# An adaLN block with an S4 convolution and a SwiGLU FFN on one core: K's rows in float32, the gate row's sum ahead of the FFN, and two moves around the first FFN step

## The chip, the core and the metric

The kernel runs on one core of a Trainium2 chip. The core has five engines, each with its own queue of instructions: TensorE (PE; its weight loads are listed apart as PEld), VectorE (DVE), ScalarE (ACT), GpSimd (POOL) and SyncE (SP), which here only issues DMAs. PE reads its operands from the on-chip memory SBUF and writes to the accumulator memory PSUM, which has eight banks. The engines wait for one another through semaphores.

The metric is the device time of one execution in microseconds (us), the median of several runs. A profiled execution has a time of its own, and a span from its first to its last instruction. Times below are us from that span's start unless they are said to be whole executions.

## The reference, cut to what matters

The input is x with 2048 rows (tokens) and 448 columns (channels). A row vector c gives six rows of 448 by `silu(c) @ w_mod`: shift, scale and gate (sa, ca, ga) for the first branch and (sb, cb, gb) for the second.

```python
mod = (_silu(c) @ w_mod).reshape(c.shape[0], 6, 1, -1)
sa, ca, ga, sb, cb, gb = (mod[:, 0], mod[:, 1], mod[:, 2], mod[:, 3], mod[:, 4], mod[:, 5])
h = _layernorm(x, axis=-1) * (1 + ca) + sa
x = x + ga * _A_ref(h, ...)      # convolution along the rows, one filter K[d, l] per channel, plus h * Dskip
h = _layernorm(x, axis=-1) * (1 + cb) + sb
x = x + gb * _B_ref(h, w_gate, w_up, w_down)   # (silu(h @ w_gate) * (h @ w_up)) @ w_down
```

The filter is `K[d, l] = Re(sum over n of C[d, n] exp(dt[d] A[d, n] l) dt[d] B[d, n])` for lags l from 0 to 2047, with 256 states n per channel.

## The kernel before, in words

**Tiles and blocks.** The 2048 rows are 16 tiles of 128, taken in six blocks of 2, 2, 3, 3, 3 and 3 tiles. For each block the FFN runs over 14 chunks of 128 hidden columns (steps 0 to 13, `gate_up(f, nw)` at L753 to L786). A step multiplies the block's normalized rows, held with channels on partitions, by the gate and up weights of its chunk, takes SiLU of the gate part on ACT (`p`, L768), multiplies on DVE (L781) and splits the product into a high and a low float32r part (`phi`, L784; `plo`, L785). `down(f - 1)` (L797) then adds the chunk before times its down weights into one PSUM bank per tile, DN[0] to DN[2]. Every float32 operand of these products is a high part rounded to float32r plus a low part with the remainder; products of high with low and low with high are added.

**Block 0 is fresh.** In it the weights arrive by DMA and are split, two steps ahead: `split_w` for the gate and up weights (high part on ACT, L123; two subtractions on DVE, L125 and L127), `split_d` for the down weights (ACT L115, DVE L117). DMA buffers for raw weights are freed by those subtractions. In steps 0 and 1 the products stand in an order by which high parts come first and low parts last.

**The first branch.** If a flag computed from A, dt and the length says that the exponents stay small, K's rows are taken as a value plus lag times a slope, one row each (k0, k1); the convolution is then a triangular matrix of ones times h * k0 plus a matrix of lag ramps times h * k1, and what passes from tile to tile is a running row (`run`). Otherwise a general path is taken, which this input does not take; after the flag all engines branch.

**The preamble.** Before the first FFN step the kernel does everything for tiles 0 and 1: six modulation rows by PE from w_mod, the sums over states for K's value and slope (DVE products, ACT sums), K's rows, the convolution of tiles 0 and 1, their second layer normalization, the transposes that put channels on partitions, and the first two weight splits. The order is written out by hand: the string PLAN is a list of names, and each name issues one small function, so the order of names is the order in every engine's queue. The names that this document uses:

- `m0`, `m1`: K's value and slope, four columns of 128 channels. `k0`, `k1` spread them to rows over all partitions (`row_of`, L371), `gdr` does so for the gated skip. `gc0`, `gc1` copy the rows to SBUF.
- `v00` to `v11`: h times k0 (v0) or k1 (v1) for tiles 0 and 1; `o00` to `o14`: their products on PE into DN[0] and DN[1], two accumulators that are the tiles' branch outputs; `hd1`, `xh1`: tile 1's skip part.
- `cp`/`ck`/`cbw`, `sp`/`sbt`/`sbc`: the rows cb and sb, summed as four groups of partitions (quads), then spread (`ck`) or turned to columns.
- `st`, `r`, `n1`, `xn`, `tr`, `hi`, `lo` with 0 or 1: for tiles 0 and 1 the second norm's statistics (DVE), reciprocal root (POOL, L167 and L168), centring (DVE), scaling (ACT, L519), transposes (PE, L391 and L394), high parts (ACT, L457) and low parts (DVE, L462).
- `w0`, `w01`, `w02`, and `w1`, `w11`, `w12`: the split of the gate and up weights of chunks 0 and 1 into high part (ACT) and two subtractions (DVE); `d00`, `d01`: the down weights of chunk 0.
- `l1`: two products whose sum the running row needs (L434); `lr0`, `lr1`: the running row's copy, sum (L439) and the small DMA that puts it in place (ACT's queue, L440); `x0`: the copy of tile 0's branch output out of DN[0].

**The gate row gb** is not in PLAN: `end_gate` runs in FFN steps 1 and 2 of block 0, five quad products (L248, L251) into the bank CV, a copy to SBUF, a spread by one product (L259) and a second copy.

Of the kernel before, what the change touches and what calls it, by code (L numbers as in the profile page):

```python
# [43 lines left out]
o10 m1 k1 cpc gd h11 hd0 v01 ck sq0 v10 cbw o12 v11 w0 o01 o02 hd1 o13 o14 xh1 gc0 sa st0 fs sp r0 n10 spc x1 xn0 gc1 st1 sbt tr0 sbc r1  # L44
fl n11 l1 hi00 xn1 w01 tr1 hi01 w02 hi1 lo0 lo1 w1 w11 d00 w12 lr0 d01 x0 lr1"""
# [11 lines left out]
def tile_kernel(ctx, tc, x, a_re, a_im, b_re, b_im, c_re, c_im, log_dt,  # L57
# [198 lines left out]
    def end_gate(z):  # L256

        if z:
            pe.matmul(CV[:, 0:D], pick.to_broadcast([128, 128]), gb, start=True, stop=True)  # L259
        else:  # L260
            mod_quads(CV, gate_w)
        sc.copy(gb, CV[:, 0:D])

# [13 lines left out]
    with tc.tile_pool(name="pre", bufs=1) as pre:  # L277
# [72 lines left out]
        ms = [pre.tile([128, 2, 4], F32R, name=f"ms{q}") for q in range(2)]  # L350
        gd2 = pre.tile([128, 2, 4], F32R, name="gd2")
# [10 lines left out]
        def parts_of(o, m, en):  # L362
            en.tensor_copy(o[:, 0], m)
            en.tensor_tensor(o[:, 1], m, f32(o[:, 0]), op=OP.subtract)

        def row_of(m, ps, last=ident2):

            for k in range(4):
                n = 128 if k < 3 else 64
                for z in range(2):  # L370
                    pe.matmul(ps[:, k * 128:k * 128 + n], m[:, z, k:k + 1].to_broadcast([128, 128]),  # L371
                              identr if k < 3 else last, start=z == 0, stop=z == 1)
# [29 lines left out]
        def gd_row():  # L402
            psm["d"] = bank()
            row_of(gd2, psm["d"], identr[:, 0:64])

        def scaled(o, a, b):
            po.tensor_tensor(o, a, b, op=OP.add)
            po.tensor_tensor(o, o, gac, op=OP.mult)
            parts_of(ms[0], o, po)

        def slope_of():
            ve.tensor_tensor(m1, a1, a2, op=OP.add)
            parts_of(ms[1], m1, ve)

        def gated_skip():
            po.tensor_tensor(gdm, vec[:, 8:12], gac, op=OP.mult)
            parts_of(gd2, gdm, po)
# [18 lines left out]
        def left_rows(z):  # L436
            e = slice(96, 128)
            if z:
                ve.tensor_tensor(run0[e], run1[e], os[1][e], op=OP.add)  # L439
# [19 lines left out]
        def low(q):  # L459
            for k in range(4):  # L460
# [13 lines left out]
        def flag_of():  # L474
# [18 lines left out]
            "m0": do(scaled, m0, m0, m0_), "m1": slope_of, "dg": gated_dt, "dga": gated_slope,  # L493
            "k0": do(row_of, ms[0], CV), "k1": do(row_of, ms[1], DN[2]), "gdm": gated_skip, "gdr": gd_row, "gd": copy(gd, lambda: psm["d"][:, 0:D]),
# [3 lines left out]
            **{n: do(quads, n[0], g) for n, g in (("gp", 2), ("cp", 4), ("sp", 3))},  # L498
# [5 lines left out]
            "cbw": lambda: sc.activation(cbw, psm["c"][:, 0:D], AF.Identity, bias=1.0),  # L504
            "sbt": lambda: turned_to(psm["s"], qt["s"]), "sbc": do(columns, sbc, "s"),
# [9 lines left out]
            "l1": left_over, **{f"lr{z}": do(left_rows, z) for z in range(2)}, "xh1": do(skip, 1), "x1": branch_1,  # L515
# [6 lines left out]
            **{f"lo{q}": do(low, q) for q in range(2)},  # L522
            "x0": copy(xs[0], os[0]),
# [200 lines left out]

    def gate_0():
# [3 lines left out]
    def run_blocks(pools, stages, first=None):  # L729
# [144 lines left out]
        for b, ts in enumerate(TILES):  # L874
            todo = {}
            if b + 1 < len(TILES):
# [221 lines left out]
```

## Time and profile before

| | |
|---|---|
| median of 3 runs | 491.31 us (489.86 to 491.55) |
| the profiled execution | 490.08 us |
| its span | 488.1 us |
| granted TensorE clock, mean over the span | 0.992 |
| PE busy | 97% of the span |
| DVE, ACT, POOL busy | 58%, 32%, 13% |
| chain that ended last | PE 93%, DMA 2%, ACT, DVE, POOL and issue 1% each |

The busy shares are means over the span. PE's records are pipelined and their ends are modelled, so two records that overlap don't mean two products at once; what a product costs is read from the start of one to the start of the next. A row of a timeline reads: start, length, engine, line, operation, output and input tiles, shape, how many in a row, and in brackets the engine's idle time before it with what ended that. The chain lists pieces with their start, length, engine, tile and line.

The span falls in three parts: the preamble up to about 35 us, block 0 of the FFN (14 steps of 3.8 us), and the five other blocks, in which PE is the bound. DMA is busy at 90% or more of its share up to the third slice of 12 us; the loads that the preamble reads are all issued at its start.

### The profile page before, as it was taken

How to read it: one execution, taken by the hardware profiler on the slowest of the kernel's cores; microseconds unless marked ns; L12 is line 12 of the kernel's file. 1: busy time of each engine (PE TensorE's matmuls, PEld its weight loads, DVE VectorE, ACT ScalarE, POOL GpSimd, SP SyncE). 2: the span in 40 equal slices, each digit the busy share in tenths (PEclk: the TensorE clock that was granted, in tenths of full speed). 3: DMA queues.
4: the chain of work that ended last, by engine and by line, in shares of the span. 5: the costliest groups of instructions: out<-in, count | busy, mean ns of one | idle time of the engine just before them, and what ended most of it. 6: DMA issues, size and time to landing. Idle time of an engine off the chain costs nothing.

```text
span 488.1 us, 7029 instructions
## 1 busy us (share of the span) xinstructions
PE 475.0 (97%) x2743; PEld 447.4 (92%) x2743; DVE 285.3 (58%) x553; ACT 155.5 (32%) x336; POOL 61.5 (13%) x86
## 2 busy tenths in 40 slices
PE   6979999999999999999999999999999999999996
PEld 4648988999998999999999999999999999999995
DVE  5877999777886536565554657364475635222225
ACT  5765645532225112232212233231222241211111
POOL 1330000000000040410004131002241000000000
PEclk9988999999999999999999999999999999999999
DMA  8953663020000200011120011130001112000001
GB/s 312 405 210 106 197 201 120 19 95 1 0 3 1 94 1 0 24 42 45 59 77 0 2 43 45 43 109 6 2 0 45 44 43 77 21 1 0 1 1 62
DMA packets 18778, 31.24 MB, mean 64 GB/s; under 512 B 2608, under 2 KB 13488, under 8 KB 18736
## 3 DMA queue, kind: packets, MB, share of 16 engines
q1 hardware_dynamic: 18000, 30.52, 18.6%
q8 instruction: 23, 0.38, 0.3%
q10 hardware_dynamic: 736, 0.19, 0.2%
q14 instruction: 19, 0.16, 0.1%
HBM read 24.61 MB, written 6.03 MB: 63 GB/s over the span
## 4 chain that ended last, share of the span: by engine, by line
PE 93%; DMA 2%; ACT 1%; DVE 1%; POOL 1%; issue 1%; DVEq 0%; POOLq 0%
PE bank L753 59%; PE dn L797 27%; DMA wm<-in_w_mod_groups_dram 2%; DMA vec<-in_c_log_dt_dram 1%; PE dn L753 1%; PE dn L483 1%; PE bank L959 1%; PE cv L958 0%; PE cv L960 0%; ACT sca L360 0%; PE bank L972 0%; POOL rsb L168 0%; DVE x L836 0%; PE bank L206 0%; PE cv L971 0%
## 5 line engine op out<-in xcount | busy, mean ns | idle before, releaser
L753 PE MATMUL bank<-hhi,gu 128*128 128x384 f32 (+1 forms) x1169 | 212.1, 320 | 0.0
L753 PEld LDWEIGHTS bank<-hhi,gu 128*128 128x128 f32 x1169 | 192.0, 189 | 3.1 <-issue 0.7
L753 PE MATMUL bank<-hlo,gu 128*128 128x384 f32 (+1 forms) x668 | 132.0, 320 | 0.0
L753 PEld LDWEIGHTS bank<-hlo,gu 128*128 128x128 f32 x668 | 110.5, 189 | 0.0
L781 DVE TENSOR_TENSOR bank<-raw,bank 128x384 f32<-128x384 f32 (+1 forms) x69 | 36.9, 534 | 125.4 <-PE bank L753 122.1
L784 ACT CAST phi<-bank 128x384 fp32r<-128x384 f32 (+1 forms) x83 | 36.8, 444 | 141.4 <-DVE bank L781 141.4
L768 ACT ACTIVATE raw<-bank 128x384 f32<-128x384 f32 (+1 forms) x70 | 32.8, 469 | 123.1 <-PE bank L753 117.1
L785 DVE TENSOR_TENSOR plo<-bank,phi 128x384 fp32r<-128x384 f32 (+1 forms) x83 | 42.4, 511 | 37.1 <-ACT phi L784 37.1
L797 PE MATMUL dn<-wdh,phi 128*128 128x448 f32 x218 | 58.3, 369 | 0.0
L797 PE MATMUL dn<-wdh,plo 128*128 128x448 f32 x218 | 57.8, 366 | 0.0
L797 PE MATMUL dn<-wdl,phi 128*128 128x448 f32 x218 | 57.6, 365 | 0.0
L797 PEld LDWEIGHTS dn<-wdl,phi 128*128 128x128 f32 x218 | 41.0, 188 | 3.4
L797 PEld LDWEIGHTS dn<-wdh,plo 128*128 128x128 f32 x218 | 40.9, 188 | 3.3
L797 PEld LDWEIGHTS dn<-wdh,phi 128*128 128x128 f32 x218 | 38.8, 188 | 2.6 <-ACT run L982 0.7
L167 POOL TENSOR_SCALAR rsb<-mvb 128x1 f32<-128x1 f32 (+2 forms) x13 | 4.6, 354 | 173.4 <-DVE mvb L151 173.4
L167 POOL TENSOR_SCALAR rsa<-mva 128x3 f32<-128x3 f32 (+1 forms) x6 | 2.4, 396 | 119.2 <-DVE mva L151 119.2
L123 ACT CAST gu<-raw 128x1024 fp32r<-128x1024 f32 x14 | 14.6, 1046 | 0.0
L125 DVE TENSOR_TENSOR gu<-raw,gu 128x768 fp32r<-128x768 f32 x14 | 13.3, 951 | 0.5 <-ACT gu L123 0.5
L933 POOL TENSOR_TENSOR m<-m,gm 128x448 f32<-128x448 f32 x9 | 10.4, 1155 | 21.4 <-DVE m L184 17.5
L947 DVE TENSOR_TENSOR vl<-m,vh 128x448 fp32r<-128x448 f32 x12 | 9.1, 756 | 6.7 <-ACT vh L946 6.1
L194 ACT ACTIVATE raw<-raw,rsb 128x64 f32<-128x64 f32 x14 | 4.8, 346 | 21.0 <-DVE raw L193 11.9
L952 POOL TENSOR_TENSOR m<-m,gd 128x448 f32<-128x448 f32 x9 | 11.5, 1282 | 0.0
(243 smaller groups left out, 418.8 us busy)
## 6 DMA issues: line engine op xcount, KB each, us to landing
raw<-in_B_w_gate_up_dram SPq DMA_DIRECT2D x14, 512.0 KB, 3.7
rawd<-in_B_w_down_dram SPq DMA_DIRECT2D x16, 224.0 KB, 4.0
x<-in_A_u_dram SPq DMA_DIRECT2D x12, 224.0 KB, 2.9
out_dram<-x SPq DMA_DIRECT2D x11, 224.0 KB, 2.0
xd<-raw SPq DMA_DIRECT2D x9, 256.0 KB, 2.0
raw<-xd SPq DMA_DIRECT2D x36, 64.0 KB, 1.9
wm<-in_w_mod_groups_dram SPq DMA_DIRECT2D x5, 448.0 KB, 8.2
wm<-in_w_mod_groups_dram SPq DMA_DIRECT2D x5, 336.0 KB, 8.2
```

The source lines that it names most:

```text
L123: sc.copy(wgu[j][:, :, 0:4, :], w)
L125: en.tensor_tensor(lo, w[:, :, 0:3, :], f32(hi), op=OP.subtract)
L167: po.tensor_scalar(rs[:, 0:n], self.mv[:, 0:n, 1], EPS, None, op0=OP.add)
L753: pe.matmul(ps[s][:, 0:n], w[:, s, a], (hlo if lo else hhi)[:, k, 0:n], start=first and q == 0, stop=end and q == len(ka) - 1)
L768: sc.activation(p[:, 0:n], ps[0][:, 0:n], AF.Silu)
L781: ve.tensor_tensor(ps[1][:, 0:n], p[:, 0:n], ps[1][:, 0:n], op=OP.mult)
L784: sc.copy(hi[:, 0:n], ps[1][:, 0:n])
L785: ve.tensor_tensor(lo[:, 0:n], ps[1][:, 0:n], f32(hi[:, 0:n]), op=OP.subtract)
L797: pe.matmul(dn[q][:, 0:D], u[:, cs], v, start=f == 0 and z == 0, stop=f == (NF - 3 if last else NF - 1) and z == 2)
L933: (ve if on_v else po).tensor_tensor(v, h, g, op=OP.mult)
L947: ve.tensor_tensor(vl, v0, f32(vh), op=OP.subtract)
L952: (ve if on_v else po).tensor_tensor(h, h, gd, op=OP.mult)
```

## The change: what it does

- **K's rows in float32.** `row_of` takes the four columns and the identity as they are, in float32, one product per group of 128 channels. Before, each column was split into a high and a low float32r part (`parts_of`: two operations, on POOL for k0 and the skip, on DVE for k1), and each group took two products with a float32r identity. The splits and the float32r identity go.
- **The gate row's sum ahead of the FFN.** `end_gate` goes. PLAN has `gq` (the five quad products, into a bank of their own), `qtb` (the copy), `gbk` (the spread) and `gb` (the second copy).
- **First weights split ahead of the second root.** `w0` moves ahead of `cbw` on ACT, and `w01`, the long subtraction, ahead of `hd1` on DVE. `w02` stays behind tile 1's centring.
- **Running row and first tile's copy inside the first FFN step.** `lr0`, `lr1` and `x0` leave PLAN; `first_rows` does the same in FFN step 0, behind `gate_up(0)` and ahead of `gate_0`.
- **Smaller moves.** `o10`, the product of v0 with a matrix of ones, goes behind `k1` and `ck`; `d00` and `d01` ahead of `w1` and `w11`; tile 0's low parts are issued in two halves.

```diff
-o10 m1 k1 cpc gd h11 hd0 v01 ck sq0 v10 cbw o12 v11 w0 o01 o02 hd1 o13 o14 xh1 gc0 sa st0 fs sp r0 n10 spc x1 xn0 gc1 st1 sbt tr0 sbc r1
+m1 k1 cpc gd h11 hd0 ck v01 sq0 o10 v10 w0 cbw o12 v11 w01 o01 o02 hd1 o13 o14 xh1 gc0 sa st0 fs sp gq r0 n10 spc x1 xn0 gc1 st1 sbt tr0
...
-    def end_gate(z):
-
-        if z:
-            pe.matmul(CV[:, 0:D], pick.to_broadcast([128, 128]), gb, start=True, stop=True)
-        else:
-            mod_quads(CV, gate_w)
-        sc.copy(gb, CV[:, 0:D])
...
-        ident2 = pre.tile([128, 64], F32R)
-        identr = pre.tile([128, 128], F32R)
-        ve.tensor_copy(identr, ident)
+        ident2 = pre.tile([128, 64], F32)
...
-        def parts_of(o, m, en):
-            en.tensor_copy(o[:, 0], m)
-            en.tensor_tensor(o[:, 1], m, f32(o[:, 0]), op=OP.subtract)
-
...
-                for z in range(2):
-                    pe.matmul(ps[:, k * 128:k * 128 + n], m[:, z, k:k + 1].to_broadcast([128, 128]),
-                              identr if k < 3 else last, start=z == 0, stop=z == 1)
+                pe.matmul(ps[:, k * 128:k * 128 + n], m[:, k:k + 1].to_broadcast([128, 128]), ident if k < 3 else last,
+                          start=True, stop=True)
...
-        def left_rows(z):
-            e = slice(96, 128)
-            if z:
-                ve.tensor_tensor(run0[e], run1[e], os[1][e], op=OP.add)
-                sc.dma_start(run[0:1], run[127:128])
-            else:
-                sc.copy(run1[e], CV[e, 0:D])
...
+            "qtb": copy(gb, lambda: psm["gq"][:, 0:D]), "gb": copy(gb, lambda: psm["gq"][:, 0:D]),
+            "gbk": lambda: pe.matmul(psm["gq"][:, 0:D], pick.to_broadcast([128, 128]), gb, start=True, stop=True),
...
+    def first_rows():
+
+        e = slice(96, 128)
+        sc.copy(run1[e], CV[e, 0:D])
+        sc.copy(xs[0], DN[0][:, 0:D])
+        ve.tensor_tensor(run0[e], run1[e], DN[1][e, 0:D], op=OP.add)
+        sc.dma_start(run[0:1], run[127:128])
+
...
                     go(EXTRA[0], gate_0)
-                    go(2, end_gate, 0)
-                    go(4, end_gate, 1)
+                    at(0, 0, first_rows)
```

How the rows stand in the engines' queues (line numbers are each kernel's own; the names after the operation are output and inputs):

PE, from K's value row to the spread of cb. `cv` takes k0, the first `bank` the skip row, `dn_70` is DN[2] with k1, `dn_68` and `dn_69` are the two tiles' accumulators. Before:

```order
L371 MATMUL cv<-identr,ms_257 128x128 x6
L371 MATMUL cv<-ident_181,ms_257 128x64 x2
L371 MATMUL bank<-identr,gd_259 128x128 x6
L371 MATMUL bank<-identr,gd_259 128x64 x2
L248 MATMUL bank<-wm_140,cs 32x448 x3
L251 MATMUL bank<-wm_140,cs 32x224 x2
L483 MATMUL dn_68<-v_0_245,tri 128x448
L513 MATMUL dn_69<-v_0_245,all_178 128x448
L371 MATMUL dn_70<-identr,ms_258 128x128 x6
L371 MATMUL dn_70<-ident_181,ms_258 128x64 x2
L400 MATMUL bank<-qtc,pick 128x448
```

The same place after:

```order
L354 MATMUL cv<-ident,m_233 128x128 x3
L354 MATMUL cv<-ident_181,m_233 128x64
L354 MATMUL bank<-ident,gdm 128x128 x3
L354 MATMUL bank<-ident,gdm 128x64
L248 MATMUL bank<-wm_140,cs 32x448 x3
L251 MATMUL bank<-wm_140,cs 32x224 x2
L449 MATMUL dn_68<-v_0_243,tri 128x448
L354 MATMUL dn_70<-ident,m_237 128x128 x3
L354 MATMUL dn_70<-ident_181,m_237 128x64
L383 MATMUL bank<-qtc,pick 128x448
L481 MATMUL dn_69<-v_0_243,all_178 128x448
```

Each row has four products for eight, and the product with all ones stands behind the slope's row and cb's spread.

DVE, from tile 0's second statistics to the weights of chunk 0 (`gu_146`). Before:

```order
L481 TENSOR_TENSOR hd_250<-h_244,gd 128x448
L150 BN_STATS stb<-dn_68 128x6
L151 BN_AGGR mvb<-stb 128x2
L466 SCALAR_TENSOR_TENSOR h_0_251<-dn_68,mvb,cbw 128x448
L452 TENSOR_TENSOR x_73<-dn_69,hd_250 128x448
L150 BN_STATS stb<-x_73 128x6
L151 BN_AGGR mvb<-stb 128x2
L397 TENSOR_REDUCE sbc<-bank 128x4
...
L466 SCALAR_TENSOR_TENSOR h_1_252<-x_73,mvb,cbw 128x448
L125 TENSOR_TENSOR gu_146<-raw,gu_146 128x2x384
L127 TENSOR_TENSOR gu_146<-raw,gu_146 64x2x128
```

And after:

```order
L447 TENSOR_TENSOR v_1_246<-h_242,dn_70 128x448
L125 TENSOR_TENSOR gu_146<-raw,gu_146 128x2x384
L447 TENSOR_TENSOR hd_248<-h_242,gd 128x448
L150 BN_STATS stb<-dn_68 128x6
L151 BN_AGGR mvb<-stb 128x2
L432 SCALAR_TENSOR_TENSOR h_0_249<-dn_68,mvb,cbw 128x448
L418 TENSOR_TENSOR x_73<-dn_69,hd_248 128x448
L150 BN_STATS stb<-x_73 128x6
L151 BN_AGGR mvb<-stb 128x2
```

The long subtraction stands ahead of tile 1's skip part, not behind its centring. The two rows left out in the first piece make the flag.

PE, from the shift row to the transposes of tile 1. Before, the five gate quads stand in step 1 (`cv<-m_79`):

```order
L248 MATMUL bank<-wm_143,cs 32x448 x3
L251 MATMUL bank<-wm_143,cs 32x224 x2
L391 MATMUL bank<-ident,qts 128x128 x3
L394 MATMUL bank<-ident,qts 64x128 x2
L391 MATMUL bank<-ident,h_0_251 128x128 x3
L394 MATMUL bank<-ident,h_0_251 64x128 x2
L434 MATMUL cv<-v_0_247,all_178 128x448
L434 MATMUL cv<-v_1_248,all_178 128x448
L391 MATMUL bank<-ident,h_1_252 128x128 x3
...
L753 MATMUL bank<-hlo,gu_148 128x256 x8
L248 MATMUL cv<-m_79,cs 32x448 x3
L251 MATMUL cv<-m_79,cs 32x224 x2
```

After:

```order
L248 MATMUL bank<-wm_143,cs 32x448 x3
L251 MATMUL bank<-wm_143,cs 32x224 x2
L248 MATMUL bank<-m_79,cs 32x448 x3
L251 MATMUL bank<-m_79,cs 32x224 x2
L374 MATMUL bank<-ident,qts 128x128 x3
L377 MATMUL bank<-ident,qts 64x128 x2
L374 MATMUL bank<-ident,h_0_249 128x128 x3
L377 MATMUL bank<-ident,h_0_249 64x128 x2
L408 MATMUL cv<-v_0_245,all_178 128x448
L408 MATMUL cv<-v_1_246,all_178 128x448
L472 MATMUL bank<-gb,pick 128x448
L374 MATMUL bank<-ident,h_1_250 128x128 x3
```

The gate's quads follow the shift's, and its spread stands between the running row's products and tile 1's transposes. On ACT the running row's copy, tile 0's copy and the DMA stood ahead of the branch to the FFN; they stand behind the first step's high part now, ahead of the next down weight's cast. On DVE the running row's sum stands behind step 0's low part and the third weights' subtractions.

More of the change, by code (lines that the diff above doesn't have):

```diff
@@ L403, in gd_row @@
             psm["d"] = bank()
[L404 removed]
+            row_of(gdm, psm["d"], ident[:, 0:64])
         def scaled(o, a, b):
@@ L1031, in tile_kernel @@
     with cond.Else():
-        for z in range(2):
-            end_gate(z)
         y = general_conv()
```

27 lines of the change are left out of this document (9 added, 18 removed).

## The prediction

> **What bounds the kernel now.** I read the page's shares and clock row first, then windows cut where the clock changes, then the chain that ended last, and last the timelines of single engines. Times are us from the span's start.
>
> ```profile
> PE 475.0 (97%) x2743; PEld 447.4 (92%) x2743; DVE 285.3 (58%) x553; ACT 155.5 (32%) x336; POOL 61.5 (13%) x86
> ...
> PEclk9988999999999999999999999999999999999999
> ```
>
> TensorE (PE) is the bound nearly everywhere, and its product count hardly changes. What can change is the start: the third and fourth slices (24 to 49 us) are where the granted clock sags. The windows of that place, and one from earlier (columns: stretch, its length, busy time of PE, PEld, DVE, ACT and POOL with their instructions, granted clock, DMA share, GB/s):
>
> ```profile
> 8.88:12.29 3.41, 2.14 (x6) 0.86 (x6) 2.71 (x4) 1.44 (x5) 0.93 (x2) 1.00 1.03 412
> 29.36:32.77 3.41, 1.99 (x15) 1.01 (x13) 2.87 (x8) 1.65 (x5) 2.06 (x2) 1.00 0.08 30
> 32.77:36.19 3.42, 2.58 (x12) 1.88 (x13) 1.51 (x6) 2.30 (x8) 0.00 (x0) 0.50 0.56 153
> 36.19:39.60 3.41, 3.41 (x18) 3.41 (x18) 3.28 (x7) 2.03 (x4) 0.00 (x0) 0.50 0.19 23
> 39.60:43.02 3.42, 3.42 (x34) 3.12 (x34) 0.92 (x2) 1.84 (x4) 0.00 (x0) 1.00 0.36 132
> ```
>
> From 32.77 to 39.60 PE runs at half clock. In the 3.41 us ahead of the drop it was busy 1.99 us, the least of these windows. The chain tells what it waited for, there and in the first FFN steps:
>
> ```profile
> 17.88 1.16 POOL ms L364
> ...
> 27.02 0.64 DVE stb L150
> ...
> 30.45 1.86 POOL rsb L168
> ...
> 32.33 0.68 ACT h L519
> ...
> 34.63 0.38 ACT hhi L457
> ...
> 47.63 0.55 ACT gb L262
> ...
> 48.23 1.02 PE cv L259 x2
> 49.24 1.21 PE dn L797 x6
> ```
>
> So the path runs through GpSimd's split of K's row (17.88), tile 1's reciprocal root (30.45), its scaling, transposes and high parts, PE at half clock, and the gate row's spread (48.23).
>
> **The change, part by part.** I follow one instant, the start of FFN step 3.
>
> *K's rows in float32.* Each row was eight float32r records and is four float32 products.
>
> ```profile
> 18.65 1.20 PE L371 MATMUL cv<-identr,ms 128*128 128x128 f32 x6
> ...
> 19.88 1.15 PE L371 MATMUL bank<-identr,gd 128*128 128x128 f32 x8
> 20.96 0.57 PE L248 MATMUL bank<-wm,cs 128*32 128x448 f32 x3
> ...
> 24.27 1.00 PE L400 MATMUL bank<-qtc,pick 128*128 128x448 f32 x2
> 25.10 0.92 PE L483 MATMUL dn<-v,tri 128*128 128x448 f32 x2
> ```
>
> A float32 product is two records (the last two rows are one product each), so a row stays eight records. Now they take (20.96 - 19.88)/8 = 0.135 each. A float32 record of 448 columns takes (25.10 - 24.27)/2 = 0.415; by columns one of 128 takes 0.12. I count the rows as equal. The ends: 8 x (0.12 - 0.135) = -0.1 a row if columns rule; 8 x (0.415 - 0.135) = +2.2 a row if a narrow record costs as much as a wide one. I take equality, because these products differ in width, and width is what separates the two prices.
>
> The gain is the wait: PE reached the first row at 18.65, and the chain has it go on only at 19.08, behind POOL's 1.16. That 0.4 shrinks to nothing since the sum was ready before 17.88. I take 0.3 (one record was already through). PE then works without a gap to the product that opens 27.02, so first statistics come at 26.7. The other splits (two POOL, two DVE operations, and the cast of the identity) lie beside PE work: 0. If that cover went, m1's split would cost some 0.4. The all-ones product of v0 goes behind the slope row and the spread; it is float32 and 448 wide before and after: 0, and PE still has all of them ahead of 27.02.
>
> *First weights split ahead of the second root.*
>
> ```profile
> 28.25 0.57 POOL L168 TENSOR_TENSOR rsb<-rsb,mhalf 128x1 f32<-128x1 f32 x1
> ...
> 30.93 0.94 DVE L125 TENSOR_TENSOR gu<-raw,gu 128x768 fp32r<-128x768 f32 x1
> 31.91 0.42 DVE L127 TENSOR_TENSOR gu<-raw,gu 64x256 fp32r<-64x256 f32 x1
> ```
>
> The same power took 0.57 for tile 0 and 1.86 for tile 1, where it ended (32.31) just as DVE's two weight subtractions did (32.33). With the long one moved ahead of hd1, the power starts at 30.45 - 0.3 = 30.15 and ends at 30.7 with tile 0's 0.57; if the short subtraction still holds it, near 31.2. ACT, though, does tile 0's first two high parts before the scaling, and these end near 31.2 either way. So the scaling starts at 31.2, not 32.33: 1.1 gained in all. The moved subtraction delays hd1 and with it the sum of tile 1 on POOL: 0.94 later than it could start, 0.1 later than now, and x1 waits behind n10 anyway: 0. The cast goes ahead of cbw on ACT, whose place was a wait for L400: 0.
>
> *The gate row's sum ahead of the FFN.* Its five quad products go behind the shift's, its spread behind l1.
>
> ```profile
> 28.98 0.55 PE L391 MATMUL bank<-ident,qts 128*128 128x128 f32 x3 [0.69 <-ACT qts L499]
> ...
> 29.82 0.55 PE L391 MATMUL bank<-ident,h 128*128 128x128 f32 x3
> ...
> 30.67 0.68 PE L434 MATMUL cv<-v,all 128*128 128x448 f32 x2
> 33.05 0.90 PE L391 MATMUL bank<-ident,h 128*128 128x128 f32 x3 [1.71 <-ACT h L519]
> ...
> 42.51 0.58 PE L248 MATMUL cv<-m,cs 128*32 128x448 f32 x3
> ...
> 43.41 0.67 PE L797 MATMUL dn<-wdh,phi 128*128 128x448 f32 x2
> ```
>
> The quads cost 43.41 - 42.51 = 0.9. They fill the 0.69 gap and the 0.3 gained ahead of it: the transposes of the shift start near 28.8, as they would have. The spread costs 0.83 (as L400) and fits the 1.71 gap: l1 ends near 31.0, the spread at 31.85, the scaled tile 1 is there at 31.9. Both are hidden; without these gaps they would cost 1.7. ACT copies the quads' sum in the time it waited for tile 0's transposes (0.5, hidden).
>
> *The clock.* With both inserted, PE has no gap over 0.5 between 25 and 36: the window that fell gets the spread's 0.83 and comes to 2.8 of 3.41, over the 2.14 of 8.88 to 12.29, which kept full clock. So I expect no drop. Tile 1's transposes start at 31.9 and take 0.85 (29.82 to 30.67) instead of 1.58 (33.05 to 34.63); high parts start at 32.85 instead of 34.63.
>
> ```profile
> 35.14:39.81 4.67, 4.67 (x22) 4.67 (x23) 3.67 (x8) 3.08 (x7) 0.00 (x0) 0.52 0.21 40
> 39.81:42.51 2.70, 2.70 (x24) 2.56 (x22) 0.43 (x1) 1.33 (x3) 0.00 (x0) 1.00 0.42 161
> ...
> 35.80 1.13 DVE L462 SCALAR_TENSOR_TENSOR hlo<-bank,sbc,hhi 128x128 fp32r<-128x128 f32 x4 [1.13 <-ACT hhi L457]
> 36.58 0.59 ACT L115 CAST wdh<-rawd 128x448 fp32r<-128x448 f32 x1
> ```
>
> FFN step 0 took 4.67 at half clock, step 1 took 2.70 at full clock for as many products. Now step 0 is bound by its operands: low parts start 1.17 after the high ones (35.80 - 34.63), at 34.0, end at 35.2, and the last eight products take 8 x 2.70/22 = 1.0: step 0 ends at 36.2, not 39.81, 3.6 earlier. That holds 0.3 + 0.8 of the two items above and 2.5 of the clock. The down weight's cast goes ahead of step 1's weights: 0.59 later on ACT and 0.63 on DVE, ready at 36.8, while step 1 wants them after six products at 36.9: 0, with 0.1 to spare.
>
> *Running row and first tile's copy.*
>
> ```profile
> 38.93 0.63 DVE L439 TENSOR_TENSOR run<-run,dn 32x448 f32<-32x448 f32 x1
> 41.65 0.43 DVE L781 TENSOR_TENSOR bank<-p,bank 128x256 f32<-128x256 f32 x1 [2.09 <-ACT p L768]
> 42.53 0.96 DVE L125 TENSOR_TENSOR gu<-raw,gu 128x768 fp32r<-128x768 f32 x1 [0.45 <-ACT gu L123]
> ...
> 44.31 0.68 DVE L727 SCALAR_TENSOR_TENSOR gm<-g,ntok,gm 128x448 f32<-128x448 f32 x1
> 46.91 0.42 DVE L781 TENSOR_TENSOR bank<-p,bank 128x256 f32<-128x256 f32 x1
> ...
> 50.29 0.99 PE L753 MATMUL bank<-hhi,gu 128*128 128x256 f32 x7
> ```
>
> Step 1 ends at 36.2 + 2.7 = 38.9, and the gate's 0.9 is not behind it. But the first down product of tile 1 writes the bank that the running row's sum reads. That sum stands on DVE behind the first multiplication, the third weights' subtractions and the low part: from 37.2 (low parts, down weight and step 1's weights done) 44.31 - 41.65 less the 0.45 of waiting = 2.2, then 0.63: 40.1. So PE waits 0.9 there; that is what is late next. Its row's DMA stands in ACT's queue behind the same sum and holds back the next down weight's cast and the next SiLU by about 1; the multiplication that wants these is at 40.1 + (46.91 - 44.31) = 42.7, so 0. Step 2 starts at 40.1 + 1.1 = 41.2 and ends at 43.8. The high part of step 1 is there at 42.7 + 0.8 = 43.5: no wait, and no spread (48.23). Down products 1.2: step 3 starts at 45.0 instead of 50.29. Weight loads on SP move with the subtractions that free their buffers: 0.
>
> **Sum.** 5.3 us: 3.6 up to step 0's end, 0.9 + 0.85 of gate products, 0.9 of wait ahead of the spread, less 0.9 of new wait. The profiled execution took 490.08 (span 488.1), so 484.8. The median of the runs is 491.31, 1.2 above it; I say 485.1.
>
> **A rule against the row.** The trace dropped the clock at 32.77 after a window 1.99/3.41 busy. The Trainium skill, page "TensorE: Matmul & The Clock Gate", Part 1, has it drop only after at least one idle window of about 3.4 us; the trace disagrees, and by that rule nothing could drop here either: 484.8. The same page's Part 4 (PE-mode transpose) says that transposes don't count as PE-busy; that speaks against the change, and the first rival is what it would do.
>
> **Rivals.** *The clock drops all the same*, because transposes don't hold it. For it: the window that dropped was only 0.15 less busy than one that kept full clock, and holds tile 0's transposes (29.82 to 30.67). Against: the quads and the spread are no transposes and add 1.7 around it. Then step 0 takes 4.67 again from 33.9 and ends at 38.55, 2.4 later; DVE's wait hides 0.6: 486.6; a whole spell of 6.83 on PE-bound work costs 3.4: 488.2. Chance 0.12.
>
> *DVE becomes the bound in block 0.*
>
> ```profile
> 50.29:69.45 19.16, 19.16 (x141) 18.70 (x140) 17.99 (x34) 11.24 (x22) 0.00 (x0) 1.00 0.66 197
> ```
>
> DVE's first multiplication moves by 41.65 - 37.2 = 4.4 and gets 0.63 more to do, so it gains 3.8 where PE gains 5.3; it has 1.17 idle here, so 0.3 to 1.5 comes back: 485.1 to 486.3. Chance 0.12.
>
> *Narrow float32 products cost as much as wide ones.* Three rows at +2.2, all ahead of 26.7: 484.8 + 6.6 = 491.4, no gain; from 0.52 a record on (24 x 0.385 = 9.2 over now's 0.135) it ends above 493.8, slower. Against: 0.415 was measured for 3.5 times the columns. Chance 0.04, half of it slower.
>
> **How the numbers follow.** My forecast has 0.7, with its own range 484.2 to 486.3 (the two baselines 490.08 and 491.31 less 5.3, with 0.3 either way for the clock's phase). The first two rivals lie at 485.1 to 488.2. With the rows' lower end (0.1 each) that makes 483.9 to 487.3 for 8 in 10. A change over 0.5% (2.5 us, about what runs of this kernel can tell from none) means below 488.85: 0.93 faster, 0.04 within, 0.03 slower.
>
> **What would show it.** Right: no half clock between 30 and 40 us; L364 gone and no gap ahead of K's first row; tile 1's power near 0.6; step 0 in about 3 us; DVE's running-row sum the releaser of the first down product of tile 1; steps 3 on at the old pace. Wrong: half clock at step 0; eight records of a K row over 1.5; PE gaps ahead of down products in steps 4 to 10; weight casts waiting for loads.

## The result, and the profile after

The changed kernel takes 485.23 us (485.06 to 485.81), the kernel before 490.64 us beside it: a ratio of 0.9891 with a 95% interval of 0.9868 to 0.9915. A second set gives 484.88 against 489.90, 0.9899 (0.9878 to 0.9920). The forecast was 485.1 in 483.9 to 487.3, so it held. The profiled execution took 485.06, its span is 483.0 (490.08 and 488.1 before).

The page of the changed kernel, its shares and its clock row:

```profile
PE 471.6 (98%) x2743; PEld 444.9 (92%) x2743; DVE 285.1 (59%) x550; ACT 155.4 (32%) x336; POOL 59.8 (12%) x82
...
PEclk9999999999999999999999999999999999999999
```

No slice sags any more, and PE is busy for 3.4 us less (475.0 before) with the same 2743 instructions. The same start, PE's timeline of the changed kernel (start, length, engine, line, tiles; in brackets the idle time before and who ended it):

```profile
18.99 1.00 PE L354 MATMUL cv<-ident,m 128*128 128x128 f32 x8
19.83 1.06 PE L354 MATMUL bank<-ident,gdm 128*128 128x128 f32 x8
...
31.04 0.92 PE L472 MATMUL bank<-gb,pick 128*128 128x448 f32 x2
32.05 0.55 PE L374 MATMUL bank<-ident,h 128*128 128x128 f32 x3
...
33.53 0.36 PE L729 MATMUL dn<-hhi,gu 128*128 128x256 f32 x1 [0.56 <-ACT hhi L423]
...
36.21 1.87 PE L729 MATMUL bank<-hhi,gu 128*128 128x256 f32 x14
...
39.20 0.47 PE L773 MATMUL dn<-wdh,phi 128*128 128x448 f32 x1 [0.17 <-ACT x L697]
40.12 0.47 PE L773 MATMUL dn<-wdh,phi 128*128 128x448 f32 x1 [0.45 <-DVE run L698]
...
45.09 0.99 PE L729 MATMUL bank<-hhi,gu 128*128 128x256 f32 x7
```

Step 0 ends at 36.21 (39.81 before), step 3 starts at 45.09 (50.29 before). Between is the new wait, 0.17 and 0.45, for ACT's copy and for DVE's sum of the running row. From step 3 to the end it is 437.9 us, as before (437.8): all of the gain is made by 45 us, and nothing of it is given back. On the other engines of the changed kernel:

```profile
30.31 0.99 POOL L168 TENSOR_TENSOR rsb<-rsb,mhalf 128x1 f32<-128x1 f32 x1
...
30.90 0.42 DVE L127 TENSOR_TENSOR gu<-raw,gu 64x256 fp32r<-64x256 f32 x1
39.45 0.63 DVE L698 TENSOR_TENSOR run<-run,dn 32x448 f32<-32x448 f32 x1
...
31.33 0.67 ACT L487 ACTIVATE h<-h,rsb 128x448 f32<-128x448 f32 x1
36.00 0.39 ACT L744 ACTIVATE p<-dn 128x256 f32<-128x256 f32 x1
```

Tile 1's root is still held, by the short subtraction alone, to 31.3; its scaling starts at 31.33 instead of 32.33. And one row that the forecast had no term for: ACT's first SiLU of the FFN stands at 36.00, where it stood at 41.18 before. The experiments turn on it.

### The profile page after: what moved, and what is told of

It is laid out like the page before. It is cut to its first block, busy times and chain, and to the rows that moved or that the text cites. A ratio compares the mean times of both kernels' runs of the same rounds, so it can differ in the third digit from the quotient of the medians.

```text
span 483.0 us, 7024 instructions
## 1 busy us (share of the span) xinstructions
PE 471.6 (98%) x2743; PEld 444.9 (92%) x2743; DVE 285.1 (59%) x550; ACT 155.4 (32%) x336; POOL 59.8 (12%) x82
## 2 busy tenths in 40 slices
DMA packets 18778, 31.24 MB, mean 65 GB/s; under 512 B 2608, under 2 KB 13488, under 8 KB 18736
## 4 chain that ended last, share of the span: by engine, by line
PE 92%; DMA 3%; DVE 2%; ACT 1%; issue 0%; POOL 0%; SPq 0%; ACTq 0%; DVEq 0%
PE bank L729 59%; PE dn L773 28%; DMA wm<-in_w_mod_groups_dram 2%; DMA x<-in_A_u_dram 1%; PE bank L238 1%; PE dn L449 1%; PE bank L934 1%; PE cv L933 1%; PE cv L935 0%; PE bank L947 0%; DVE x L812 0%; PE bank L206 0%; PE cv L946 0%; PE cv L948 0%; ACT raw L195 0%
```

## The experiments

First each part is undone in the changed kernel (e1 to e4), then the clock is tried in the kernel before (e5, e6); e9 to e12 follow from what these showed, and e7 is an attempt at a better version, with the changed kernel beside it (e8).

### The gate row's products back in the FFN (e1)

```diff
-m1 k1 cpc gd h11 hd0 ck v01 sq0 o10 v10 w0 cbw o12 v11 w01 o01 o02 hd1 o13 o14 xh1 gc0 sa st0 fs sp gq r0 n10 spc x1 xn0 gc1 st1 sbt tr0
-qtb sbc r1 fl n11 l1 gbk hi00 xn1 w02 tr1 hi01 lo00 hi1 lo01 lo1 d00 d01 w1 w11 gb w12"""
+m1 k1 cpc gd h11 hd0 ck v01 sq0 o10 v10 w0 cbw o12 v11 w01 o01 o02 hd1 o13 o14 xh1 gc0 sa st0 fs sp r0 n10 spc x1 xn0 gc1 st1 sbt tr0
+sbc r1 fl n11 l1 hi00 xn1 w02 tr1 hi01 lo00 hi1 lo01 lo1 d00 d01 w1 w11 w12"""
...
+                    go(2, end_gate, 0)
+                    go(4, end_gate, 1)
```

> The changed kernel with one part undone: the products of the gate row's sum and spread go back into the first and second FFN steps, as they stood before the change. Against 485.2 us for the changed kernel and 490.6 for the kernel before. Theory (TensorE's clock follows the share of a window that it works; the split of the first weights ahead of the root and the float32 rows have already shortened the gaps): the preamble's tail stays at full clock, the five products come back into the FFN with 0.9 + 0.85 us and some tenths of waiting behind them, so 487.0 to 487.8. Rival (the five products in the gaps are what held the clock): a half-clock spell from about 32 us returns and costs some 2.4 us more, so 489 to 490. Second rival (they hide in the FFN's waits as well as in the gaps): 485.2.

Measured: 486.30 us (486.09 to 486.61), 0.9931 of the kernel before (0.9914 to 0.9947), 1.1 to 1.4 above the changed kernel. PE of this kernel, and the window in which the kernel before had been at 1.99 (columns as in the prediction's windows):

```profile
39.98 0.74 PE L779 MATMUL dn<-wdh,phi 128*128 128x448 f32 x2
...
44.27 1.02 PE L259 MATMUL cv<-gb,pick 128*128 128x448 f32 x2
...
46.34 0.99 PE L735 MATMUL bank<-hhi,gu 128*128 128x256 f32 x7
```

```profile
29.13:32.54 3.41, 2.55 (x19) 1.44 (x18) 2.18 (x8) 2.51 (x7) 1.21 (x2) 1.00 0.19 54
```

The clock stays full without the inserted products: the rival falls. The two down products at 39.98 no longer wait, since the quads (39.09 to 39.98) stand in the place of the wait for DVE's sum. Step 2 then starts at 41.36, only 0.1 later than in the changed kernel (its loads came 0.13 later), so the quads cost nothing more; the spread and its wait for ACT's copy make up the other 1.15 of the 1.25 between the two starts of step 3 (46.34 and 45.09).

### The first weights' long subtraction back behind the second centring (e2)

```diff
-m1 k1 cpc gd h11 hd0 ck v01 sq0 o10 v10 w0 cbw o12 v11 w01 o01 o02 hd1 o13 o14 xh1 gc0 sa st0 fs sp gq r0 n10 spc x1 xn0 gc1 st1 sbt tr0
-qtb sbc r1 fl n11 l1 gbk hi00 xn1 w02 tr1 hi01 lo00 hi1 lo01 lo1 d00 d01 w1 w11 gb w12"""
+m1 k1 cpc gd h11 hd0 ck v01 sq0 o10 v10 w0 cbw o12 v11 o01 o02 hd1 o13 o14 xh1 gc0 sa st0 fs sp gq r0 n10 spc x1 xn0 gc1 st1 sbt tr0
+qtb sbc r1 fl n11 l1 gbk hi00 xn1 w01 w02 tr1 hi01 lo00 hi1 lo01 lo1 d00 d01 w1 w11 gb w12"""
```

> The changed kernel with the first split of the FFN's weights (the long subtraction on VectorE) put back behind the second tile's centring. Theory: POOL's second root is again held by it, its power takes about 1.9 us instead of 0.99, the second tile's scaling starts at about 32.2 instead of 31.33, the clock stays full, and the third FFN step starts 0.8 to 1.0 us later: 486.0 to 486.3. Rival A (the root isn't on the path): 485.2. Rival B (the longer gap is enough for the clock to drop): a half-clock spell costs 2 to 3 us more, 488 to 489.

Measured: 485.04 us (484.88 to 485.95), the changed kernel's time. But the run did not bring back what it was to bring back. POOL, DVE and ACT of this kernel:

```profile
30.28 0.57 POOL L168 TENSOR_TENSOR rsb<-rsb,mhalf 128x1 f32<-128x1 f32 x1
...
31.14 0.94 DVE L125 TENSOR_TENSOR gu<-raw,gu 128x768 fp32r<-128x768 f32 x1
...
31.30 0.67 ACT L487 ACTIVATE h<-h,rsb 128x448 f32<-128x448 f32 x1
```

The power is over at 30.85, 0.29 before the subtraction starts at 31.14, and it takes 0.57. In the kernel before it started at 30.45, the subtraction at 30.93, 0.48 later, and it was held to 32.3; e5, e6, e9 and e10 below, which have the split in its old place too, have the same 0.48 and a power of 1.84 or 1.85. Here the subtraction started 0.86 after the power, because DVE idled 0.28 ahead of a small reduction, for no cause that the trace shows. So the root was not late here and the run does not price a late one. The other three executions took 484.97 to 485.95 and have no trace.

### K's rows in float32r pairs again (e3)

```diff
-pe.matmul(ps[...], m[:, k:k + 1].to_broadcast([128, 128]), ident if k < 3 else last, start=True, stop=True)
+for z in range(2):
+    pe.matmul(ps[...], m[:, z, k:k + 1].to_broadcast([128, 128]), identr if k < 3 else last, start=z == 0, stop=z == 1)
...
+parts_of(ms[0], o, po)
...
+parts_of(ms[1], m1, ve)
...
+parts_of(gd2, gdm, po)
```

> The changed kernel with K's rows made as before, each from two float32r parts that are split on POOL and VectorE. Theory: the float32 rows cost TensorE about as much as the pairs (eight records in 0.84 us), and their gain is only the wait for POOL's split, so 0.2 to 0.5 us slower: 485.4 to 485.7. Rival (narrow float32 products are dearer than the pairs): faster than the changed kernel, 484.5 to 485.0.

Measured: 485.45 us (484.69 to 486.32), 0.9913 (0.9894 to 0.9932). The scatter doesn't part it from the changed kernel; the chain of waits does. Of this kernel:

```profile
18.08 1.16 POOL ms L356
19.24 0.04 issue
19.28 0.97 PE cv L363 x7
20.25 0.99 PE bank L363 x8
...
27.23 0.64 DVE stb L150
```

POOL's split is back on the chain, the first statistics come at 27.23 instead of 26.87, step 3 starts at 45.40 instead of 45.09. The part is worth 0.3 to 0.4, all of it a wait; the pairs' row takes 0.99 in the chain, the float32 row 0.89 (19.99 to 20.88 in the changed kernel). A narrow float32 record costs no more than a float32r one, and the rival falls.

### The running row ahead of the loop again (e4)

```diff
-qtb sbc r1 fl n11 l1 gbk hi00 xn1 w02 tr1 hi01 lo00 hi1 lo01 lo1 d00 d01 w1 w11 gb w12"""
+qtb sbc r1 fl n11 l1 gbk hi00 xn1 w02 tr1 hi01 lo00 hi1 lo01 lo1 d00 d01 w1 w11 gb w12 lr0 x0 lr1"""
...
-                    at(0, 0, first_rows)
```

> The changed kernel with the running row's copy, sum and transfer and the first tile's copy put back at the end of the preamble, ahead of the loop. Theory: the wait of the second down product for VectorE's sum is gone, but ScalarE's copies and the transfer that it issues stand ahead of the first branch of the FFN, so that branch is 2 to 3 us later and the step's multiplication with it; the third step starts some 1.5 us later, 486.2 to 487.2. Rival (ScalarE has room there, only the wait goes): 0.5 to 0.9 us faster, 484.3 to 484.7.

Measured: 487.75 us (487.07 to 489.33), 0.9961 (0.9950 to 0.9973), 2.5 to 2.9 above the changed kernel: beyond the theory's range on its own side, and opposite to the rival. ACT's rows of this kernel, the row of its flag's load (duration in ns, then start), and PE's:

```profile
37.77 0.61 ACTq L414 DMA_DIRECT2D run<-run  x1
39.36 0.38 ACT L752 ACTIVATE p<-dn 128x256 f32<-128x256 f32 x1 [2.35 <-PE bank L737]
```

```profile
L511 ACTq TENSOR_LOAD <-flag x1: 708/708/708, 38.4 to 38.4; - x1
```

```profile
41.00 0.67 PE L781 MATMUL dn<-wdh,phi 128*128 128x448 f32 x2 [2.06 <-ACT phi L768]
```

ACT's queue is in order. The transfer waits for DVE's sum (37.77), takes 0.61 to issue, and only behind it comes the load of the flag on which the engine branches into the loop, 0.71, then the first SiLU. The releaser that the row names, a bank of PE, had been done for long. PE waits 2.06 for the product of that SiLU. In the changed kernel the same load runs beside the high parts and costs nothing; there it reads

```profile
L503 ACTq TENSOR_LOAD <-flag x1: 472/472/472, 33.0 to 33.0; - x1
```

Part of the difference is the clock: in the profiled execution it falls at 42.18 for one window, behind this gap. The two executions with a mean clock of 0.999 took 487.07 and 487.38, about where the theory put it.

### Extra work for PE in the kernel before (e5, e6)

```diff
-fl n11 l1 hi00 xn1 w01 tr1 hi01 w02 hi1 lo0 lo1 w1 w11 d00 w12 lr0 d01 x0 lr1"""
+fl n11 l1 fill hi00 xn1 w01 tr1 hi01 w02 hi1 lo0 lo1 w1 w11 d00 w12 lr0 d01 x0 lr1"""
...
+            "fill": lambda: pe.matmul(DN[2][:, 0:D], f32(all1), v0[0], start=True, stop=True),
```

and in e6, in place of that product:

```diff
+            "fill": lambda: [pe.transpose(DN[2][:, k % 3 * 128:k % 3 * 128 + 128], h2[0][:, k % 3 * 128:k % 3 * 128 + 128], ident) for k in range(7)],
```

> The kernel before with one float32 product of 448 columns added, into a bank that nobody reads, in TensorE's gap of 1.71 us ahead of the second tile's turning; nothing else is changed, and the output doesn't use it. Theory (the clock fell because TensorE worked only 1.99 of 3.41 us ahead of the drop): with about 0.9 us more the spell at half clock doesn't come, and the kernel is faster though it computes more: 487.8 to 488.8 against 490.6. Rival (the drop has another cause, or needs a share higher still): the spell stays, 490.6 to 491.

> The kernel before with seven transposes of the first tile's rows added in the same gap, into the same bank, about as long as the product; the output doesn't use them. Theory (transposes are work like any other for the clock): as with the product, 487.8 to 488.8. Rival (transposes don't count as work for the clock): the spell stays, and the time is 490.6 to 491.

Measured: with the product 489.92 us (489.22 to 491.30), 0.9993 (0.9978 to 1.0008); with the transposes 490.97 us (490.56 to 491.77), 1.0018 (1.0005 to 1.0030). Both did what they were to do to the clock: the mean clock was 0.997 or more in 8 of 10 executions with the product and in 10 of 10 with the transposes, against 2 of the 23 of the kernel before beside them. And neither was faster. Of the kernel with the product, PE and ACT:

```profile
37.22 1.82 PE L754 MATMUL bank<-hhi,gu 128*128 128x256 f32 x14
...
42.20 0.67 PE L798 MATMUL dn<-wdh,phi 128*128 128x448 f32 x2 [1.31 <-ACT phi L785]
...
49.68 0.99 PE L754 MATMUL bank<-hhi,gu 128*128 128x256 f32 x7
...
38.97 0.61 ACTq L440 DMA_DIRECT2D run<-run  x1
40.56 0.38 ACT L769 ACTIVATE p<-dn 128x256 f32<-128x256 f32 x1 [2.90 <-PE bank L754]
```

Step 0 ends at 37.22 instead of 39.81, so the spell's 2.6 us are saved. Then PE waits 1.31 for the product of the SiLU at 40.56, which stood at 41.18 with the spell; step 3 starts at 49.68, 0.6 earlier. My theory on record falls: the spell was real, its price was not on the path, because the running row's transfer held ACT just as long. The kernel before shows it too: its seven executions with a clock of 0.999 (five beside e1 to e4, two beside e9 to e12) took 489.2 to 489.9.

The run with the transposes answers a rule: the Trainium skill, "TensorE: Matmul & The Clock Gate", Part 4, says that a transpose in TensorE's transpose mode doesn't count as PE-busy the same way. Here transposes do count: ten executions kept the clock with nothing added but transposes (the profile lists them as MATMUL and does not show a mode). Its time is 1.0 above the product's although its step 3 starts at 49.50; the profile has the running row's transfer in the second block land later (DVE waits 1.25 for it at 138.84). Why it does was not tried.

### The row's move alone, and with the product (e9, e10)

```diff
-fl n11 l1 hi00 xn1 w01 tr1 hi01 w02 hi1 lo0 lo1 w1 w11 d00 w12 lr0 d01 x0 lr1"""
+fl n11 l1 hi00 xn1 w01 tr1 hi01 w02 hi1 lo0 lo1 w1 w11 d00 w12 d01"""
...
+                    at(0, 0, first_rows)
```

That is e9, the kernel before with `first_rows` of the changed one; e10 has `fill` behind `l1` as e5 besides.

> The kernel before with one part of the change alone: the running row's copy, sum and transfer and the first tile's copy move from the end of the preamble into the first FFN step. Theory after the earlier runs (neither the clock nor the row is a price by itself: TensorE at half clock and ScalarE's late first branch end at about the same time, so either alone hides the other): where the half-clock spell comes, the second step still starts at about 44.7, and only the gate row's spread gets earlier, by some 0.7 us: 489.0 to 489.9 against 489.9. Rival (the row's place costs 2 us whatever the clock does, as its return did in the changed kernel): 487.5 to 488.

> The kernel before with the same move and, besides, the one added product of 448 columns that kept the clock up. Theory (the two are worth something only together): step 0 ends at 37.2, the first branch no longer waits for the transfer, the second step starts at about 42.5 and the third at 47.3 instead of 50.29, so 486.8 to 487.4, 2.5 to 3 us faster, though the added product alone gave nothing and the move alone gives at most 0.9. Rival (something else in the first steps holds them): 488.5 to 489.5.

Measured: the move alone 486.76 us (486.57 to 487.26), 0.9940 (0.9916 to 0.9964); with the product 487.53 us (486.59 to 490.10), 0.9958 (0.9939 to 0.9977). The first lies below both expectations, because the clock held in all four executions (0.998), with nothing inserted and the 1.70 gap still there. Of the move alone, ACT's SiLU, PE's step 3, and the two windows around the gap:

```profile
36.56 0.38 ACT L767 ACTIVATE p<-dn 128x256 f32<-128x256 f32 x1 [0.45 <-PE dn L752]
...
46.64 0.99 PE L752 MATMUL bank<-hhi,gu 128*128 128x256 f32 x7
```

```profile
28.51:31.93 3.42, 2.37 (x16) 1.32 (x16) 3.25 (x9) 1.66 (x5) 2.06 (x2) 1.00 0.18 66
31.93:35.34 3.41, 2.17 (x17) 1.79 (x18) 1.72 (x7) 2.90 (x8) 0.00 (x0) 1.00 0.45 154
```

The gap is shared out between two windows of 2.37 and 2.17, where the kernel before had one of 1.99. The other corner is in the ten executions of the second kernel: two with a lower mean clock (0.991 and 0.994), which speaks for a spell though neither was traced, took 490.10 and 489.94, the other eight (0.997 to 1.000) 486.6 to 488.1. The traced one is of the eight; PE's third product with w_mod, which waits for a load, and step 3:

```profile
15.11 1.02 PE L238 MATMUL bank<-wm,cs 128*128 128x448 f32 x2 [0.17 <-DMA wm<-in_w_mod_groups_dram]
...
47.41 1.00 PE L753 MATMUL bank<-hhi,gu 128*128 128x256 f32 x7
```

So:

| | spell at half clock | clock full |
|---|---|---|
| row ahead of the loop | 489.9 (kernel before, median) | 490.3 (e5, middle of the eight at 0.997 or more) |
| row in step 0 | 490.0 (e10, two executions, not traced) | 486.8 (e9), 487.4 (e10, middle of eight) |

Neither alone gives anything; both together give 2.5 to 3.1 us.

### The row, the product and the split (e11)

The same as e10, and `w01` behind `w0` (`... v11 w0 w01 o01 ...`), as the change has it.

> The same as the run above, and the first weights' long subtraction ahead of the second root as in the change. Theory of the forecast (the root, held to 32.3 by VectorE's two subtractions, is on the path): the second tile's scaling at 31.4 instead of 32.32, and all behind it 0.8 to 0.9 earlier: 486.0 to 486.5. Rival (the root isn't on the path, as the run with the split put back may say): as the run above, 486.8 to 487.4.

Measured: 489.31 us (487.64 to 490.33), 0.9981 (0.9965 to 0.9997): 1.8 slower than e10, against both theories. DVE and ACT of this kernel, and its window:

```profile
27.22 0.96 DVE L125 TENSOR_TENSOR gu<-raw,gu 128x768 fp32r<-128x768 f32 x1 [1.19 <-ACT gu L123]
...
30.80 0.67 ACT L512 ACTIVATE h<-h,rsb 128x448 f32<-128x448 f32 x1 [1.48 <-POOL rsb L168]
```

```profile
29.29:32.70 3.41, 2.09 (x16) 1.33 (x17) 3.23 (x10) 1.34 (x4) 2.32 (x5) 1.00 0.13 47
32.70:36.11 3.41, 3.29 (x11) 1.58 (x9) 1.38 (x5) 1.56 (x6) 0.22 (x1) 0.50 0.54 148
```

I had moved the subtraction and not the cast that it needs: in the change `w0` goes ahead of `cbw` on ACT, here it stayed behind it. DVE waited 1.19 for the cast, the skip part behind it was late, POOL's sum with it, and tile 0's root, next in POOL's queue, so that tile 0 was scaled at 30.80 instead of 29.17 (e10). The clock then fell as well. The run does not price the split, then, and it shows that the cast's place is part of the edit. It does show what the moved subtraction does to tile 1's root. POOL of e10 and of this kernel:

```profile
30.76 1.84 POOL L168 TENSOR_TENSOR rsb<-rsb,mhalf 128x1 f32<-128x1 f32 x1
```

```profile
32.00 0.92 POOL L168 TENSOR_TENSOR rsb<-rsb,mhalf 128x1 f32<-128x1 f32 x1
```

Tile 1's scaling starts 5.31 after the first statistics in e10 (27.32 to 32.63) and 4.37 after them here (28.63 to 33.00).

### The row ahead of the loop, its transfer on SyncE (e12)

Against e4:

```diff
-                sc.dma_start(run[0:1], run[127:128])
+                sy.dma_start(run[0:1], run[127:128])
```

> The changed kernel with the running row and the first tile's copy ahead of the loop, as in the run that put them back, but with the transfer issued on SyncE's queue instead of ScalarE's. Theory (what held the first branch there was the transfer on ScalarE: it waits for VectorE's sum, and the loading of the branch's flag stands behind it, 0.65 us of transfer and 0.94 us of load and branch, before the first SiLU): that SiLU comes at about 37.1 instead of 39.36, the second step starts at about 40.2 without a wait, and the time is 484.0 to 484.8, at least as fast as the changed kernel. Rival (the copies and the sum themselves are what is late there): 486 to 487.8, as when ScalarE issued it.

Measured: 487.51 us (486.30 to 488.19), 0.9943 (0.9920 to 0.9967): the rival's number, by neither mechanism. ACT and SP of this kernel:

```profile
36.53 0.39 ACT L752 ACTIVATE p<-dn 128x256 f32<-128x256 f32 x1
43.61 1.04 ACT L123 CAST gu<-raw 128x1024 fp32r<-128x1024 f32 x1 [4.63 <-DMA raw<-in_B_w_gate_up_dram]
...
37.39 0.63 SPq L414 DMA_DIRECT2D run<-run  x1
39.34 1.39 SPq L105 DMA_DIRECT2D raw<-in_B_w_gate_up_dram  x3
```

The theory's half is right: with the transfer off ACT's queue the SiLU comes at 36.53, and step 2 starts at 39.74 without a wait (42.88 in e4). But now SP's queue stands behind DVE's sum, the next gate and up weights are asked for at 39.34 instead of 37.25 (SP's own load of the flag, 0.71 long, stands behind the transfer too, at 38.1), and ACT waits 4.63 for them. The wait has only changed its queue. The clock, which falls for one window behind that wait, is not the whole reason: the two executions with a clock of 1.000 took 486.30 and 486.44, still 1.1 to 1.6 above the changed kernel.

### The row's sum early, the gate multiplication late (e7), beside the changed kernel (e8)

```diff
-EXTRA = (1,)
+EXTRA = (3,)
...
-qtb sbc r1 fl n11 l1 gbk hi00 xn1 w02 tr1 hi01 lo00 hi1 lo01 lo1 d00 d01 w1 w11 gb w12"""
+qtb sbc r1 fl n11 l1 gbk hi00 xn1 w02 tr1 hi01 lr0 lo00 hi1 lo01 lr1 lo1 d00 d01 w1 w11 gb w12"""
...
+                sy.dma_start(run[0:1], run[127:128])
```

`lr0` and `lr1` are the copy and the sum with the transfer, as in the kernel before; of `first_rows` only the first tile's copy is left in step 0. `EXTRA` is the half-step in which `gate_0` is issued.

> The changed kernel with the running row's copy and sum moved into the preamble, each between two of the low halves' operations, its transfer on SyncE's queue instead of ScalarE's, only the first tile's copy left in the first step, and the multiplication of the gate row moved from half-step 1 to half-step 3. Theory: the second down product of the second tile no longer waits for VectorE's sum, and ScalarE isn't held by the transfer, for about 0.1 us more in the low halves: 0.4 to 0.9 us faster, 484.3 to 484.8. Rival (VectorE's multiplication of the second step ends last, whatever stands ahead of it): 485.2.

> The changed kernel itself, on the same chip and beside the run above, so that the two are compared by the same runs: 485.2, as it measured.

Measured: 484.00 us (483.85 to 484.39) against 484.88 (484.71 to 486.90) for the changed kernel on the same chip, both against 489.90: 0.9871 (0.9851 to 0.9891) and 0.9899. Here the sum runs at 33.60 on DVE and the transfer is issued at 34.26, early enough that SP asks for weights at 36.21. PE of this kernel:

```profile
38.94 0.57 PE L777 MATMUL dn<-wdh,phi 128*128 128x448 f32 x2
...
43.99 1.00 PE L733 MATMUL bank<-hhi,gu 128*128 128x256 f32 x7
```

No wait ahead of the down products, and step 3 at 43.99 against 44.82 in the changed kernel beside it. The theory holds (0.88 faster, with 0.4 to 0.9 expected), and this version is ahead of both kernels. What the later multiplication gave and what the row gave was not tried apart.

## Why the prediction was right

**K's rows, 0.3.** Right: first statistics 0.33 earlier once the loads' 0.18 is taken out (26.87 against 27.02), and 0.3 to 0.4 by e3. That rows in float32 cost as much as the pairs was right to 0.1.

**The first weights' split, 0.8.** Right. The scaling came at 31.33 (31.2 forecast), held as foreseen to 31.3 by the short subtraction and by ACT's two high parts (in e4 the power was over at 30.75, and the scaling still started at 31.23). From the first statistics to this scaling it is 5.31 or 5.32 in the kernel before, e5, e6, e9 and e10, and 4.44 to 4.55 in the changed kernel, its repeat e8 and e1, e3, e4, e7 and e12; e1 is without the early gate products and e3 without the float32 rows. Only e2 is short (4.46) with the split in its old place, by DVE's stall. So it is the split's place that frees the root.

**The gate row, 0.9 + 0.85, hidden.** Both fit the gaps: the transposes of tile 1 start at 32.05 (31.9 forecast), their operand ready at 32.0. Undone, they cost 1.25, nearly all of it the spread: the quads would have stood where PE now waits, so that in the sum 0.9 gained and 0.9 of new wait were one and the same place.

**No drop of the clock.** Right in the trace, and for a weaker reason than I gave: the two insertions weren't needed (e1 keeps the clock without them). What does keep it is not shown: e9 kept it in four executions with the old order of the preamble.

**The step that failed** is the clock's term: "That holds 0.3 + 0.8 of the two items above and 2.5 of the clock." Step 0 does end 2.6 earlier when the clock is kept (e5: 37.22 against 39.81), but by itself that moves step 3 by 0.6 and the time by nothing that can be measured. The other side of the same error is the running row, which the forecast has only as a cost ("PE waits 0.9 there"): its move is the condition for those 2.5 us. With the clock full it brings step 3 from 49.68 (e5) to 47.41 (e10, whose loads were 0.3 later), and put back into the changed kernel it costs 1.9 to 2.5 us in the two executions whose clock was 0.999 (487.07 and 487.38 against 484.9 to 485.2).

What each term was worth can be read at the start of step 3. It is counted from the third product with w_mod (L238), which waits for a load, so that loads that land earlier or later drop out:

| kernel | L238 | step 3 | between |
|---|---|---|---|
| before | 14.80 | 50.29 | 35.49 |
| clock full (e5) | 14.79 | 49.68 | 34.89 |
| and the row in step 0 (e10) | 15.11 | 47.41 | 32.30 |
| and K's rows, split and smaller moves, without the added product (e1) | 15.10 | 46.34 | 31.24 |
| and the gate row (changed kernel) | 14.98 | 45.09 | 30.11 |

The clock alone gave 0.60, the row behind it 2.59, K's rows and the split 1.06 (0.3 + 0.8 forecast), the gate row 1.13. The forecast had 2.5 for the clock and no gain for the row, 0.7 too little for the two together, and 1.75 for the gate row with both its waits (0.9 + 0.85 + 0.9 - 0.9), 0.6 too much. Each row is one trace, and in another order the first two steps would share their 3.2 otherwise.

Why the sum was right all the same: it was not made of prices of parts. It followed one instant through the changed order, and in that order the transfer stood behind step 0's SiLU, so that its hold on ACT never entered: step 0 at 36.2 (36.21), step 2 at 41.2 (41.26), step 3 at 45.0 (45.09). DVE's running-row sum was forecast to end at 40.1; it ends at 40.08. What the forecast had overlooked in the kernel before is ACT's transfer and flag load (39.59 to 41.1), hidden there by PE at half clock: the SiLU's product was ready at 42.8, and PE came to it at 43.41. So the forecast was right on the path of the changed kernel and wrong on what had held the kernel before. Its range was also worked out with a slip: 490.08 less 5.3 less 0.3 is 484.5, not 484.2.

**The rivals.** The clock did not drop. DVE did not become the bound: from step 3 on the two kernels take the same 437.8 and 437.9. Narrow float32 products cost 0.105 to 0.124 a record.

## What to carry to other kernels

Two delays that end at the same time hide each other: each undone alone gives next to nothing, and the forecast of a change that undoes both must follow the schedule, not add up prices; to learn what each is worth, run all four combinations. A small transfer that waits holds everything behind it in its engine's queue, the load of a branch's flag too, and on another engine's queue it holds what that one issues; in e7, where its input is ready early, nothing that counts waits behind it. A moved instruction takes along what it waits for (e11).

## What the runs showed of the hardware

**The clock.** It is granted in windows of 3.41 us, counted from its first rise (the kernel before: 8 windows full, 2 half; e4: 11 full, 1 half; e12: 12 full, 1 half), and that rise lies between 4.4 and 6.7 us after the start in these profiles, so the same code meets the windows at different places. Windows ahead of a drop, of e4 and of e12:

```profile
38.77:42.18 3.41, 1.34 (x7) 0.80 (x6) 1.87 (x4) 2.82 (x6) 0.00 (x0) 1.00 0.33 131
```

```profile
42.05:45.47 3.42, 0.98 (x7) 0.76 (x6) 1.44 (x3) 1.86 (x4) 1.12 (x2) 1.00 0.93 362
```

and one early in the changed kernel, behind which the clock stayed:

```profile
7.81:11.22 3.41, 1.74 (x4) 0.68 (x4) 2.50 (x4) 0.57 (x4) 1.72 (x2) 1.00 1.03 415
```

With 1.99 in the kernel before and 2.09 in e11, the windows ahead of a drop were 29 to 61% busy (the drop at the program's end, behind work that has run out, left aside). Around the FFN's start, windows of 2.11 (e5), 2.17 (e9) and 2.21 (e6) kept the clock; but with 1.74 kept as well, and 2.07 near the end of e12, a threshold near 2.1 of 3.41 is not the whole rule. The Trainium skill, "TensorE: Matmul & The Clock Gate", Part 1, has the clock drop after at least one idle window of about 3.4 us. The window's length agrees, its idleness does not.

**GpSimd's power beside VectorE's subtraction.** The power of one column takes 0.57 when the subtraction starts 0.23 or 0.29 after its end (e4, e2). When the subtraction starts 0.02 to 0.11 after the point where those 0.57 would be over, the power takes 0.99 to 1.08 and ends with the subtraction (the changed kernel, e7, e12); in the kernel before it started 0.09 ahead of that point, and the power took 1.85, to the end of the second subtraction behind it (the scaling that needs it started at 32.33). Centring, which runs beside it on DVE in all of these, doesn't hold it. The Trainium skill, "SBUF — State Buffer", section "SBUF: two separate sides", has whichever of the two starts first, a GpSimd operation or a VectorE one with two SBUF inputs, keep the shared port pair for its whole instruction; here the power started first each time and was the one held.
